# Preparation's products on VectorE and four more filler matmuls per unit, in a fused recurrent-attention and mixture-of-experts kernel

## The chip, the cores and the metric

One core of a Trainium2 chip runs the whole program. The metric is the device time in microseconds (us) of one execution, the median of three runs. Five engines work side by side, each with its own in-order queue: TensorE (PE, matmuls and weight loads), VectorE (DVE), ScalarE (ACT), GpSimd (POOL) and SyncE (SP, which here issues most DMA transfers). An instruction at the head of a queue that waits holds up everything behind it in that queue.

## The reference

Attention is a recurrence over 768 tokens for 4 batches and 8 heads with a 40x40 state per head; its output is the input of a mixture of 8 experts with the best two chosen per token.

```python
for t in range(S):
    y[:, :, t] = np.einsum('bhd,bhde->bhe', rt, state)
    Sa = np.einsum('bhde,bhe->bhd', state, at)
    state_decay = state * wt[:, :, None, :] - np.einsum('bhd,bhe->bhde', Sa, bt)
    state = state_decay + np.einsum('bhd,bhe->bhde', vt, kt)
...
logits = x @ w_gate
noisy_logits = logits + np.log1p(np.exp(x @ w_noise)) * noise
top2 = np.argpartition(-noisy_logits, 2, axis=1)[:, :2]
...
h = np.maximum(x[mask] @ w1[e], 0.0)
out[mask] += top2_w[mask, k, None] * (h @ w2[e])
```

## The kernel before

Attention is computed in chunks of 64 tokens. A **unit** is one chunk of one half `p` (two batches, 8 heads); there are 12 chunks and 2 halves, so 24 units, and they run one after another because the state of a half passes from chunk to chunk. Two chunks of both halves (four units) are a **group**; there are six groups, 0 to 5.

Each group is prepared ahead of its units, once per half. `prepA` scans the decays (`Gx`, L495), takes logarithm and exponential on ScalarE, and forms `NH` and `NG_` (L506). It multiplies `b` by `NH` (L518) and `a` by `NG_` (L520), and after each product `pack` splits the result into two 16-bit halves: ScalarE first (L459), then VectorE (L460), then a DMA. `prepC` does the same for `k`, with two products of half width (L544). `scoresL` multiplies the packed matrices on TensorE, and `tsolve` inverts 32x32 triangles by 30 steps of two vector instructions (L570, L571). The solves of groups 0 and 1 run on VectorE, those of groups 2 to 5 on GpSimd (`TPOOL`); a DMA brings the result back as `T`.

In the kernel before, the products of L518 and L520 run on VectorE for groups 0 and 1 and on GpSimd for groups 2 to 5 (`MD=(0,1)`); those of L506 run on GpSimd for all groups (`MG=()`); those of L544 run on VectorE for group 0 alone (`MK=(0,)`). Group 1's VectorE work goes through the wrapper `Behind` and shows under L399.

A unit has three parts. `chain` applies `T` twice to what the state and the chunk give (tile `pQ`), sums the new state in `pS` and writes it (L667). `outp` forms the attention output (`psc`, `pY`, L680, L691). `Moe.logits` transposes that output (`px`, L97), splits it on ScalarE and VectorE (`xT`, L98, L99) and multiplies it by the gate's weights with nine narrow matmuls (`pl`, L101). `route` and `place` follow for every few units. The experts (`hidden` L287, `output` L309) run after the last unit.

Fillers are matmuls whose result nobody reads: `warm` (L596) multiplies a constant by a constant, 320 columns each, into a PSUM tile that the next real matmul starts anew. Before, there are two per unit, in front of the first application of `T` (`ND=(2,0,0,0)`).

The order of instructions on each engine is not the order of the code. A scheduler simulates the program and issues on each engine what its model finds ready first, with priorities from the code; `burst` keeps runs of matmuls together. A change in one place therefore moves instructions everywhere in attention. PSUM tiles of one tag share buffers: `pl`, `pgm`, `pg`, `pr`, `pn` and the scores of `scoresL` share the single buffer of tag `pp`.

Of the kernel before, what the change touches and what calls it, by code (L numbers as in the profile page):

```python
# [8 lines left out]
F32 = mybir.dt.float32  # L9
# [30 lines left out]
class Moe:  # L40
# [51 lines left out]
    def logits(s,n,xt,ps,tag,bufs=(1,1)):  # L92

        nc=s.nc
        s.xw=s.xws[n]=nc.sync.dma_start(s.xd[n>=NA][128*n:128*n+128],xt)
        px=ps.tile([128,3,128],F32,name="px",tag=tag[0],bufs=bufs[0])
        s.burst([lambda k=k,c0=c0: nc.tensor.transpose(px[:,k],xt[:,c0:c0+128],s.idm) for k,c0 in enumerate((0,128,192))])  # L97
        xT=s.rp.tile([128,2,3,128],F16,name="xT",tag="xT",bufs=2); nc.scalar.activation(xT[:,0],px,AF.Copy,scale=XS)  # L98
        nc.vector.scalar_tensor_tensor(xT[:,1],px,XS,xT[:,0],op0=ALU.mult,op1=ALU.subtract)  # L99
        pl=ps.tile([128,16],F32,name="pl",tag=tag[1],bufs=bufs[1])  # L100
        s.burst([lambda i=i,a=a,b=b,k=k: nc.tensor.matmul(pl,xT[:,a,k],s.wg[:,b,k],start=i+k==0,stop=i+k==4) for i,(a,b) in enumerate(((0,0),(1,0),(0,1))) for k in range(3)])  # L101
        if n==0: s.n0=0
        j=n-s.n0
        if j==0: s.lg=s.rp.tile([128,RT,16],F32,name="lg")
        nc.scalar.activation(s.lg[:,j],pl,AF.Copy,scale=1/(XS*WS))
        if j==s.rts[0]-1:
            s.route(s.n0,s.rts.pop(0),ps,tag[1],bufs[1])
            if n<NA: s.nc.sync.dma_start(s.xd[1][128*s.n0:128*n+128].rearrange("(p a) f->p (a f)",p=128),s.xd[0][128*s.n0:128*n+128].rearrange("(p a) f->p (a f)",p=128))
            s.n0=n+1
            if n+1==NA: s.turn()  # L110
# [293 lines left out]
class Att:  # L404
# [234 lines left out]
    def chain(s,p,cc,o):  # L639
# [19 lines left out]
        s.ul=nc.scalar.activation(s.Ut[:,:,0:40],U,AF.Copy,scale=-IS)  # L659
        if not last:  # L660
            Sp=s.psb.tile([128,8,40],F32,name="pS",tag="pacc",bufs=s.PACC)
            if first: f=[s.mm(Sp,s.idh,s.dm,start=True,stop=False,skip_group_check=True)]
            else: f=[s.mm(Sp,s.ids,sfs[:,l],start=l==0,stop=False,skip_group_check=True) for l in range(2)]
            s.burst(f)
            s.burst([s.mm(Sp[64*b:64*b+40,h],o['kb'][:,b,h],vu[:,b,h],start=False,stop=True,skip_group_check=True) for h,b in HB(1)])
            gb=s.gam[p][:,0:8,cc+1:cc+2].to_broadcast([128,8,40])
            nc.vector.scalar_tensor_tensor(s.Sst[p][:,:,0:40],Sp,IS,gb,op0=ALU.mult,op1=ALU.mult)  # L667
# [80 lines left out]
TB=4  # L748
EW=(1,1)
MB=2  # L750
ND=(2,0,0,0)

BB=1

# [11 lines left out]

BAB=1; RKB=1
SAB=5
MD=(0,1); MG=(); MK=(0,); TG=0
GA=-1; GC=-1  # L770
def HB(k=0): return [(h,b^k) for h in range(8) for b in range(2)]

# [90 lines left out]
def build(nc,tc,A,out):  # L863
    with ExitStack() as ctx:
        m=Moe(nc,tc,ctx,(A['wgn'],A['nz'],A['w1'],A['w2'],out))
        with ExitStack() as c2:
            s=Att(nc,tc,c2,(A['fm'],A['vt'],A['fm2'],A['rv']))
            m.burst=s.burst; s.run(m)
            m.flag(s.ps,"pt",s.PT,s.mags)
        with ExitStack() as c2:  # L870
            m.pools(c2)
            m.experts(s.sd0.ins)
        F=Any_(nc,tc,m,{z:A['raw_'+z] for z in 'rkvwab'},A['nzr'])
        rv=nc.values_load(m.fl[0:1,1:2],min_val=0,max_val=1)
        with tc.If(rv>0):
            with ExitStack() as c2:
                m.pools(c2); m.extra()
            r2=nc.values_load(m.fl[0:1,0:1],min_val=0,max_val=1)
            with tc.If(r2>0):
                F.run()  # L880
# [17 lines left out]
```

## Time and profile before

| | us |
|---|---|
| median of 3 runs | 1052.31 (1048.45 to 1052.65) |
| profiled execution | 1041.7 |
| its span, first to last instruction | 1039.9 |
| PE / PEld busy in the span | 819.7 / 716.3 |
| DVE / ACT / POOL busy | 543.8 / 389.8 / 399.2 |

Durations come from the profiled execution, which was 10.6 us shorter than the median of the runs. "Busy" counts an engine's instructions and not its waits. PEclk is the clock that TensorE was granted, as a share of 2.4 GHz; 0.50 is its lower level, 1.2 GHz. From about 90 us the units run, from about 616 us the experts. In rows of the trace, `out<-in` names what an instruction writes and reads, and a bracket or a second bar gives the idle time in front of it with the instruction that ended it.

### The profile page before, as it was taken

The numbers are of one execution on the slowest core, as the hardware profiler recorded it, in microseconds if no ns is written. First come the engines' busy times: TensorE is split into PE (matmuls) and PEld (weight loads), VectorE is DVE, ScalarE is ACT, GpSimd is POOL, SyncE is SP. The second block draws the span as 40 slices with busy tenths as digits, with TensorE's granted clock in tenths as the row PEclk, the third lists the DMA queues.
The fourth block names the chain that finished last, engine by engine and source line by source line (L and its number), as shares of the span: only waits on it lengthen the run. The fifth ranks groups of instructions, "written<-read, shape, count | busy, mean of one in ns | idle before, by whom it ended". The sixth has DMA issues, their size and how long they took to land.

```text
span 1039.9 us, 27444 instructions
## 1 busy us (share of the span) xinstructions
PE 819.7 (79%) x11706; PEld 716.3 (69%) x11706; DVE 543.8 (52%) x1150; ACT 389.8 (37%) x820; POOL 399.2 (38%) x504
## 2 busy tenths in 40 slices
PE   0113456769888758888988789999999999999994
PEld 0113345557666646777766668899899999999994
DVE  9268568554469774338554753633443434343420
ACT  2202333335445433444442432525243535343420
POOL 6102241167659778219301004335151516160312
PEclk9999998779869866988996789999999999999998
DMA  4793996387588484473494402435252525252303
GB/s 119 177 235 91 254 249 152 93 226 198 124 213 249 126 206 110 110 160 108 138 280 147 135 14 43 120 93 133 58 133 67 131 64 133 61 137 59 35 8 37
DMA packets 127111, 135.88 MB, mean 131 GB/s; under 512 B 59249, under 2 KB 106805, under 8 KB 126901
## 3 DMA queue, kind: packets, MB, share of 16 engines
q1 hardware_dynamic: 116292, 114.90, 41.4%
q0 software_dynamic: 10688, 19.14, 9.7%
q8 instruction: 94, 1.54, 0.6%
q14 instruction: 37, 0.30, 0.1%
HBM read 96.25 MB, written 41.03 MB: 132 GB/s over the span
## 4 chain that ended last, share of the span: by engine, by line
PE 50%; POOL 13%; DMA 13%; DVE 11%; issue 5%; ACT 3%; SPq 2%; POOLq 0%; ACTq 0%; DVEq 0%
PE ph L287 17%; PE po L309 17%; POOL X L571 4%; POOL Tt L570 4%; DMA d_ab<-pk 3%; DMA rawk<-in_fm_dram 3%; PE psc L470 3%; PE pY L470 2%; PE pt L268 2%; PE pQ L470 2%; DVE X L571 1%; DVE Tt L570 1%; PE pW L470 1%; DMA d_k<-pk 1%; DMA X<-scr 1%
## 5 line engine op out<-in xcount | busy, mean ns | idle before, releaser
L311 POOL DMA_INDIRECT out_dram<-y,oi x56 | 92.2, 1647 | 233.7 <-ACT y L310 212.2
L290 DVE SCALAR_TENSOR_TENSOR hl<-ph,hh 128x256 fp32r<-128x256 f32 (+1 forms) x128 | 70.1, 555 | 120.4 <-ACT hh L288 113.2
L288 ACT ACTIVATE hh<-ph 128x320 fp32r<-128x320 f32 (+1 forms) x128 | 64.6, 518 | 147.7 <-PE ph L287 140.4
L470 PE MATMUL pQ<-w,T 32*32 32x40 f32 x2304 | 49.5, 229 | 48.4 <-ACT w L473 23.7
L470 PEld LDWEIGHTS pQ<-w,T 32*32 32x32 f32 x2304 | 42.2, 133 | 61.8 <-ACT w L473 26.3
L309 PE MATMUL po<-w2h,hh 128*128 128x320 f32 x384 | 74.8, 314 | 2.5 <-DVE y L304 1.9
L470 PE MATMUL psc<-RV,uT 128*64 128x128 f32 x384 | 65.3, 325 | 12.6 <-DVE P L680 12.1
L571 POOL TENSOR_TENSOR X<-X,Tt 128x30 f32<-128x30 f32 (+14 forms) x120 | 72.0, 600 | 8.2
L252 POOL DMA_INDIRECT xr<-xd,gi x56 | 53.7, 958 | 51.2 <-DVE oi L178 17.8
L309 PE MATMUL po<-w2h,hl 128*128 128x320 f32 x384 | 70.8, 311 | 0.0
L287 PE MATMUL ph<-xh,w1h 128*128 128x512 f32 (+1 forms) x256 | 69.7, 355 | 1.1 <-DVE hl L290 1.1
L570 POOL TENSOR_TENSOR Tt<-X 128x30 f32<-128x30 f32 (+14 forms) x120 | 67.2, 560 | 7.8
L287 PE MATMUL ph<-xh,w1l 128*128 128x512 f32 (+1 forms) x256 | 68.9, 350 | 0.0
L287 PE MATMUL ph<-xl,w1h 128*128 128x512 f32 (+1 forms) x256 | 68.6, 349 | 0.0
L470 PEld LDWEIGHTS psc<-RV,uT 128*64 128x64 f32 x384 | 51.7, 164 | 22.9 <-DVE P L680 13.0
L309 PE MATMUL po<-w2l,hh 128*128 128x320 f32 x384 | 65.7, 309 | 0.0
L309 PEld LDWEIGHTS po<-w2h,hh 128*128 128x128 f32 x384 | 61.0, 188 | 6.7 <-issue 2.3
L470 PE MATMUL psc<-RV 128*64 128x128 f32 x384 | 65.3, 325 | 0.0
L680 DVE TENSOR_TENSOR P<-psc,mk 128x512 f32<-128x512 f32 x48 | 32.9, 686 | 59.1 <-PE psc L470 59.1
L309 PEld LDWEIGHTS po<-w2h,hl 128*128 128x128 f32 x384 | 59.8, 188 | 0.5
L470 PEld LDWEIGHTS <-st_ab 120*64 120x64 f16 (+1 forms) x928 | 28.3, 123 | 44.1 <-issue 30.5
L309 PEld LDWEIGHTS po<-w2l,hh 128*128 128x128 f32 x384 | 58.6, 188 | 0.1
(314 smaller groups left out, 1936.2 us busy)
## 6 DMA issues: line engine op xcount, KB each, us to landing
w2r<-in_w_dram SPq DMA_DIRECT2D x8, 1280.0 KB
RV<-in_rv_dram SPq DMA_DIRECT2D x48, 192.0 KB
rawba<-in_fm_dram SPq DMA_DIRECT2D x24, 360.0 KB
d_ab<-pk SPq DMA_DIRECT2D x24, 360.0 KB
st_ab<-d_ab SPq DMA_DIRECT2D x36, 240.0 KB
w1r<-in_w_dram SPq DMA_DIRECT2D x8, 1024.0 KB
raww<-in_fm_dram SPq DMA_DIRECT2D x12, 365.6 KB
st_ab<-d_ab SPq DMA_DIRECT2D x24, 180.0 KB
```

The source lines that it names most:

```text
L252: k=t//128; nc.gpsimd.indirect_dma_start(out=X[:p,k if s.cap==CAP else 0],out_offset=None,in_=s.xd[int(w is not s.early[0])],in_offset=OFF ...
L268: for t,p in tiles(t0,n): nc.tensor.transpose(pt[:,t-t0:t-t0+p],x[:p,t//128,f0:f0+128],s.idm[:p,:p])
L287: for i,(a,b) in enumerate(mm): nc.tensor.matmul(ph[:,:n],a,b,start=i==0,stop=i==7)
L288: nc.scalar.activation(hh[:,f,:n],ph[:,:n],AF.Relu)
L290: if c.stop>c.start: nc.vector.scalar_tensor_tensor(o,ph[:,c],0.0,hh[:,f,c].bitcast(F32),op0=ALU.max,op1=ALU.subtract)
L309: s.lm=nc.tensor.matmul(po[:p],h[:,f,r],w[:,f],start=k==0,stop=k==23); k+=1
L311: st=nc.gpsimd.indirect_dma_start(out=s.out_d,out_offset=OFFS(ap=idx[:p,e,ii:ii+1],axis=0),in_=y[:p],in_offset=None,compute_op=ALU.add)
L470: def mm(s,*a,**k): return lambda: s.nc.tensor.matmul(*a,**k)
L570: eng.tensor_tensor(t,Xt[:,j:j+1,j+1:].to_broadcast([128,j,m]),Xt[:,0:j,j:j+1].to_broadcast([128,j,m]),op=ALU.mult)
L571: s.tl=eng.tensor_tensor(Xt[:,0:j,j+1:],Xt[:,0:j,j+1:],t,op=ALU.add)
L680: nc.vector.tensor_tensor(m,pp.rearrange("p i j t->p (i j) t"),s.mk.to_broadcast([128,8,64]),op=ALU.mult)
```

## The change

Two things are changed. First, the products of L506, L518, L520 and L544 all run on VectorE: 12 of L506 (all groups), 8 of L518 and 8 of L520 (groups 2 to 5), and 20 half-width ones of L544 (groups 1 to 5) leave GpSimd. With `0 in MG` the gate's constants are also no longer ordered behind `s.pl`, the last of group 0's L506. Second, `WN=(3,1)` adds fillers: three in front of the logits' product, written to the unused 320 columns of the widened tile `plw`, and one in front of the state's sum `pS`. That is 24 x 3 and 22 x 1, 94 in all.

```diff
-        pl=ps.tile([128,16],F32,name="pl",tag=tag[1],bufs=bufs[1])
+        plw=ps.tile([128,336],F32,name="pl",tag=tag[1],bufs=bufs[1]); pl=plw[:,0:16]
+        s.warm(plw[:,16:336],WN[0])
...
             Sp=s.psb.tile([128,8,40],F32,name="pS",tag="pacc",bufs=s.PACC)
+            s.warm(Sp,WN[1])
...
-ND=(2,0,0,0)
+ND=(2,0,0,0); WN=(3,1)
...
-MD=(0,1); MG=(); MK=(0,); TG=0
+MD=MG=MK=range(6); TG=0
...
-            m.burst=s.burst; s.run(m)
+            m.burst=s.burst; m.warm=s.warm; s.run(m)
```

Two lines are added to the code, so L518 of before is L519 of the changed kernel, L506 is L507, L544 is L545, and L596 is L597.

On GpSimd, at the preparation of group 4's second half (`NG__4427`), which stands among the first steps of group 3's solve (`Tt` and `X` are the solve's tiles, `rawba` holds `b` and `a`), the order before is:

```order
L571 TENSOR_TENSOR X<-X,Tt 128x2x29
L506 TENSOR_TENSOR NG__4427<-Gx,raww 120x768
L570 TENSOR_TENSOR Tt<-X 128x84
L571 TENSOR_TENSOR X<-X,Tt 128x3x28
L570 TENSOR_TENSOR Tt<-X 128x108
L518 TENSOR_TENSOR rawba<-rawba,NH 120x768
L571 TENSOR_TENSOR X<-X,Tt 128x4x27
L520 TENSOR_TENSOR rawba<-rawba,NG__4427 120x768
```

The same steps of that solve in the changed kernel:

```order
L572 TENSOR_TENSOR X<-X,Tt 128x2x29
L571 TENSOR_TENSOR Tt<-X 128x84
L572 TENSOR_TENSOR X<-X,Tt 128x3x28
L571 TENSOR_TENSOR Tt<-X 128x108
L572 TENSOR_TENSOR X<-X,Tt 128x4x27
L571 TENSOR_TENSOR Tt<-X 128x130
L572 TENSOR_TENSOR X<-X,Tt 128x5x26
```

The three products have left the solve, whose steps follow each other.

On VectorE, at the end of the same preparation, the order before is (`pk` is the packed half, `Sst` the state, `xT` the split output):

```order
L680 TENSOR_TENSOR P<-psc,mk 128x512
L658 TENSOR_SCALAR vu<-pQ 64x320
L691 TENSOR_TENSOR xt<-pY,xt 128x320
L606 TENSOR_TENSOR ak<-psc,mk_127 128x512
L460 SCALAR_TENSOR_TENSOR pk<-rawba,pk 120x768
L667 SCALAR_TENSOR_TENSOR Sst_169<-pS,gam_148 128x8x40
L99 SCALAR_TENSOR_TENSOR xT<-px,xT 128x384
L460 SCALAR_TENSOR_TENSOR pk<-rawba,pk 120x768
```

In the changed kernel, there (`NG__4467` is this preparation's `NG_`, `rawk` holds `k`):

```order
L545 TENSOR_TENSOR rawk<-rawk,NH 120x6x64 x2
L461 SCALAR_TENSOR_TENSOR pk<-rawba,pk 120x768
L682 TENSOR_TENSOR P<-psc,mk 128x512
L507 TENSOR_TENSOR NG__4467<-Gx,raww 120x768
L521 TENSOR_TENSOR rawba<-rawba,NG__4467 120x768
L461 SCALAR_TENSOR_TENSOR pk<-rawba,pk 120x768
L682 TENSOR_TENSOR P<-psc,mk 128x512
L461 SCALAR_TENSOR_TENSOR pk<-rawk,pk 120x2x384
L659 TENSOR_SCALAR vu<-pQ 64x320
```

Two `pk` were all that VectorE had of this preparation there; now the products stand between the units' own work (`P`, `vu`), each in front of the `pk` that needs it.

On TensorE, at a unit's logits in the middle of attention (`pn` is a step of routing, `idh` and `dm` the filler's constants), before:

```order
L165 MATMUL pn<-ohB,ohA 128x256
L97 MATMUL px<-idm,xt 128x128 x3
L471 MATMUL pd<-idf,Sst_170 128x128 x4
L101 LDWEIGHTS xT
L101 MATMUL pl<-wg,xT 128x16
```

and in the changed kernel:

```order
L166 MATMUL pn<-ohB,ohA 128x256
L97 MATMUL px<-idm,xt 128x128 x3
L472 MATMUL pd<-idf,Sst_170 128x128 x4
L597 LDWEIGHTS idh
L597 MATMUL pl<-dm,idh 128x320
```

The last two rows are the first filler, with its own weight load; two more follow it, then the logits' product with `xT`, which stood there before.

## Rows read from the trace of the kernel before

**Rows 1.** The windows view by stage of the program. Columns: stretch in us from the span's start, its length, then busy us (and instructions) of each engine, the granted TensorE clock, the busy share of the DMA engines, GB/s.

```profile
200.00:616.00 416.00, 339.67 (x7760) 279.82 (x7760) 236.01 (x517) 173.89 (x414) 209.22 (x312) 0.82 0.61 160
616.00:1040.00 424.00, 404.98 (x2460) 373.53 (x2458) 172.03 (x373) 160.62 (x298) 142.27 (x110) 0.99 0.35 81
```

**Rows 2.** From the page: busy time of each engine in the span, and the chain that ended last, shares of the span by engine.

```profile
PE 819.7 (79%) x11706; PEld 716.3 (69%) x11706; DVE 543.8 (52%) x1150; ACT 389.8 (37%) x820; POOL 399.2 (38%) x504
...
PE 50%; POOL 13%; DMA 13%; DVE 11%; issue 5%; ACT 3%; SPq 2%; POOLq 0%; ACTq 0%; DVEq 0%
```

**Rows 3.** The waits of ScalarE (ACT) from 100 to 620 us: who waited for whom, us in total, times, longest.

```profile
ACT pk L459 <- POOL rawba L518: 38.4, 8, 7.7
...
ACT pk L459 <- POOL rawba L520: 8.3, 6, 3.6
...
ACT pk L459 <- POOL rawk L544: 5.0, 1, 5.0
```

**Rows 4.** The timeline of ScalarE from 375 to 386 us: start, duration, line, operation, output from input, and in brackets the idle time in front and its releaser.

```profile
382.64 0.84 ACT L459 ACTIVATE pk<-rawba 120x768 f16<-120x768 f32 x1 [7.16 <-POOL rawba L518]
...
384.28 0.44 ACT L473 ACTIVATE w<-pW 128x320 f32<-128x320 f32 x1
```

**Rows 5.** The timeline of GpSimd (POOL) from 380 to 383 us.

```profile
380.38 0.48 POOL L570 TENSOR_TENSOR Tt<-X 128x168 f32<-128x168 f32 x1
380.81 1.80 POOL L518 TENSOR_TENSOR rawba<-rawba,NH 120x768 f32<-120x768 f32 x1
382.57 0.54 POOL L571 TENSOR_TENSOR X<-X,Tt 128x168 f32<-128x168 f32 x1
```

**Rows 6.** The timeline of TensorE (PE) at five places, one row each: first matmuls after a wait.

```profile
174.15 1.27 PE L470 MATMUL pQ<-w,T 32*32 32x40 f32 x32 [6.31 <-ACT w L473]
...
228.49 0.25 PE L101 MATMUL pl<-wg,xT 128*128 128x16 f16 x3 [6.30 <-ACT xT L98]
...
269.92 0.76 PE L470 MATMUL pW<-q,lo 32*32 32x40 f32 x32 [1.76 <-ACT q L652]
...
303.64 0.25 PE L101 MATMUL pl<-wg,xT 128*128 128x16 f16 x3 [3.03 <-ACT xT L98]
...
384.77 1.28 PE L470 MATMUL pQ<-w,T 32*32 32x40 f32 x32 [6.72 <-ACT w L473]
```

**Rows 7.** The windows view again, in stretches of 8 us behind three of those waits (columns as in rows 1).

```profile
224.00:232.00 8.00, 3.44 (x43) 2.92 (x44) 5.69 (x6) 3.26 (x7) 7.85 (x7) 0.50 0.94 210
...
304.00:312.00 8.00, 6.88 (x122) 5.43 (x124) 5.85 (x14) 3.24 (x9) 6.37 (x9) 0.50 1.00 247
...
384.00:392.00 8.00, 4.36 (x86) 3.62 (x88) 7.94 (x9) 4.05 (x9) 7.84 (x8) 0.50 0.62 164
...
392.00:400.00 8.00, 6.22 (x99) 5.54 (x99) 5.08 (x7) 1.67 (x4) 7.05 (x10) 0.50 0.67 178
...
400.00:408.00 8.00, 7.34 (x121) 5.47 (x121) 1.80 (x3) 2.44 (x6) 6.71 (x9) 0.50 0.29 73
```

**Rows 8.** TensorE's timeline at two places: two filler matmuls (L596) and the matmuls that follow, at the low clock (400 to 405 us) and at the high one (433 to 435 us).

```profile
402.66 0.71 PE L596 MATMUL pQ<-dm,idh 128*128 128x320 f16 x2
...
404.03 1.22 PE L470 MATMUL pQ<-w,T 32*32 32x40 f32 x60 [0.66 <-ACT w L473]
...
433.79 0.45 PE L596 MATMUL pQ<-dm,idh 128*128 128x320 f16 x2
...
434.16 0.79 PE L470 MATMUL pQ<-w,T 32*32 32x40 f32 x64
```

**Rows 9.** What one product costs on either engine: for a line, the count, min/median/max in ns, first and last start, forms. L518 multiplies `b` by `NH`, L544 half of `k`.

```profile
L518 POOL TENSOR_TENSOR rawba<-rawba,NH x8: 1799/1804/1946, 119.7 to 380.8; 120x768 f32<-120x768 f32 x8
...
L518 DVE TENSOR_TENSOR rawba<-rawba,NH x2: 946/952/959, 14.1 to 24.8; 120x768 f32<-120x768 f32 x2
...
L544 POOL TENSOR_TENSOR rawk<-rawk,NH x20: 985/1007/1942, 91.9 to 401.8; 120x384 f32<-120x384 f32 x20
...
L544 DVE TENSOR_TENSOR rawk<-rawk,NH x4: 549/553/557, 39.5 to 47.3; 120x384 f32<-120x384 f32 x4
```

**Rows 10.** VectorE's group of L504 from 90 to 616 us, a product of the form of L518 that VectorE has done all along (shapes, count, busy us, mean ns, idle in front); then VectorE's timeline at 372 us and GpSimd's at 370 us, two instructions that ran at the same time.

```profile
L504 DVE TENSOR_TENSOR NH<-raww,Gx 120x768 f32<-120x768 f32 x8 | 11.5, 1443 | 0.1
...
372.57 2.76 DVE L504 TENSOR_TENSOR NH<-raww,Gx 120x768 f32<-120x768 f32 x1
...
370.35 4.17 POOL L564 TENSOR_TENSOR X<-X,tri 128x1024 f32<-128x1024 f32 x1 [5.37 <-DMA X<-scr]
```

**Rows 11.** TensorE's groups from 90 to 616 us: line, tiles, count, busy us, mean ns, and after the second bar the idle time in front with what ended it. L101 is the logits' product.

```profile
L101 PE MATMUL pl<-wg,xT 128*128 128x16 f16 x216 | 11.9, 174 | 21.3 <-ACT xT L98 13.1 <-DVE xT L99 6.5 <-DVE tab L166 0.6
```

**Rows 12.** The waits of GpSimd for DMA from 100 to 620 us.

```profile
POOL rawk L544 <- DMA rawk<-in_fm_dram: 34.0, 7, 18.8
...
POOL rawba L518 <- DMA rawba<-in_fm_dram: 6.5, 2, 4.0
```

**Rows 13.** GpSimd's timeline: first product and closing transfer of the solve for group 3, and the same for group 5.

```profile
291.26 2.13 POOL L564 TENSOR_TENSOR X<-X,tri 128x1024 f32<-128x1024 f32 x1 [6.89 <-DMA Vz<-in_vt_dram]
...
354.28 0.62 POOL L573 DMA_DIRECT2D scr<-X  x1 [0.32 <-POOL X L571]
...
463.85 2.13 POOL L564 TENSOR_TENSOR X<-X,tri 128x1024 f32<-128x1024 f32 x1 [39.81 <-DMA X<-scr]
...
504.65 0.59 POOL L573 DMA_DIRECT2D scr<-X  x1 [0.30 <-POOL X L571]
```

## The prediction

> **What bounds the kernel now.** I read the windows by stage first. From 616 us on, in the experts, TensorE is busy 404.98 of 424 us at a granted clock of 0.99 [rows 1]; the change adds and moves nothing there, so I leave that stage as it is. From 200 to 616 us, in attention, TensorE is busy 339.67 of 416 us and its clock is 0.82, while VectorE is busy 236.01 and GpSimd 209.22 [rows 1]. No engine is full. Time is lost in two ways there: TensorE waits 76 us (416 less 340), and it works part of the time at its lower clock. A mean of 0.82 between the levels 1.0 and 0.5 means that 36% of the stretch, some 150 us, ran at the lower one. The chain that ended last gives the same picture: TensorE half of the span, GpSimd 13%, VectorE 11%, ScalarE 3% [rows 2].
>
> Next I asked who makes TensorE wait, and read ScalarE's waits. The largest that has to do with the change is `pk` (L459), which waits for the products on GpSimd: 38.4 us for L518, 8.3 us for L520 and 5.0 us for L544, together 51.7 us [rows 3]. The reader can follow one of them in the timelines. GpSimd was in the middle of a solve and came to L518 only at 380.81, for 1.80 us [rows 5]. ScalarE stood at `pk` for 7.16 us until 382.64, and `w`, which is the unit's own work, was queued behind it and ran at 384.28 [rows 4]. TensorE, which needed `w`, stood for 6.72 us [rows 6]. The solve's own lateness is not what is waited for here; a short product behind it in a queue is.
>
> **The change part by part. Stalls removed.** With the products on VectorE, GpSimd has only solve steps and routing sums, and `pk` no longer waits for it. Five waits of TensorE follow such a stop of ScalarE: 6.31, 6.30, 1.76, 3.03 and 6.72 us, 24.1 us in all [rows 6]. The bounds are 0 (something else is late at the same moment) and 51.7 (all that ScalarE waited [rows 3]); I take the 24.1, which is what reached TensorE in one piece, and 18% of the other 27.6, 5 us, because TensorE waits 18% of the stage (76 of 416) and these ten stops of ScalarE may show in its shorter waits. That is 29 us.
>
> **Cold work removed.** Behind three of these waits the clock is at 0.50 for five stretches, in which TensorE is busy 3.44 + 6.88 + 4.36 + 6.22 + 7.34 = 28.2 us [rows 7]. The same narrow matmuls take 1.22 us per 60 there and 0.79 us per 64 at the high clock [rows 8], a ratio of 0.61. At the high clock the 28.2 us would be 17.2, a gain of 11. Over the whole stage the most to be had so is 150 us x 0.82 busy x 0.39 = 48 us, and the least is 0. Each 0.01 of the mean clock is 2.7 of these 48 us. I take a mean of 0.88 for a TensorE that idles less and has fillers, which is 16 us: the 11 and 5 more.
>
> **VectorE's new work.** It gets 28 products of 768 columns and 20 of 384. One takes 0.952 us and 0.553 us on VectorE where nothing else is in its way, against 1.804 and 1.007 on GpSimd [rows 9]: 26.7 + 11.1 = 37.7 us. L504 has the same form as the wide one and is run by VectorE already, partly beside a solve; its mean is 1.443 us [rows 10]. By that factor of 1.52 the sum is 57.2 us. Work on VectorE costs nothing where VectorE would have idled, and all of it where a unit waits for `vu`, `P` or `Sst` behind it, so 0 and 57.2 are the ends. The chain gives VectorE 11% of 1039.9 us, 114 us, of 543.8 busy [rows 2], so 21% of its time is on the path; 21% of 37.7 to 57.2 is 8 to 12, and I take 10. On what the two engines do to each other, the trace shows L504 at 2.76 us while GpSimd's L564 ran 4.17 us [rows 10], where L564 takes 2.13 us elsewhere [rows 13]. The Trainium skill, "SBUF — State Buffer", section "Who interferes with whom", says why: a VectorE instruction with two SBUF inputs and a GpSimd instruction that reads SBUF share a read interface, and whichever begins first keeps it to its end. The trace agrees as to a long wait on both sides. By that rule the change trades a late product for a blocked one, and the 57.2 is the likelier sum; that rule's case is the second rival.
>
> **Waits for DMA that change engine.** On GpSimd, L544 waited 34.0 us for `rawk` and L518 6.5 us for `rawba` [rows 12]; on VectorE the same wait would hold the units' own work. The largest, 18.8 us [rows 12], was in an empty stretch of GpSimd and would move with the order; 21.7 us are left. I take VectorE's 21% of that, 5 us; the ends are 0 and 21.7.
>
> **The solve.** Without products among its steps it is shorter: group 3's went from 291.26 to 354.28, 63 us with the preparation of group 4 in it, group 5's from 463.85 to 504.65, 41 us with none [rows 13]. I cost that at nothing. Group 3's result left at 354.28 [rows 13], and units still worked on for tens of us; the wait at 384.77 was for `w` and not for `T` [rows 6]. If another thing removed that slack, 22 us per solve would count.
>
> **Fillers.** There are 94. Two of them take 0.71 us at the low clock and 0.37 at the high one (433.79 to 434.16) [rows 8], so 0.355 and 0.185 each; at the stage's mix of clocks (36% low) 0.246, together 23 us. They stand in front of the logits' product, where TensorE waited 21.3 us in all [rows 11]. Of those, 6.30 and 3.03 are stalls already counted as removed [rows 6], so 12 us are left to fill, and 11 us are uncovered. With no cover at all the cost is 23 (up to 33 if everything were cold), with full cover 0; fillers that keep the clock up pay some of it back, which is in the 5 above. The order on GpSimd and the startup are the remaining edits: `NG_` of group 0 on VectorE and the constants issued earlier are worth 1 us either way, and I count 0.
>
> **The sum.** 29 + 16 - 10 - 5 - 11 = 19 us less. The profiled execution took 1041.7 us, so it would be 1022.7. The median before, 1052.31, is 10.6 above that execution, so for the median I add 10.6 and forecast 1033 us, 1.8% less.
>
> **The rivals.** First, the clock follows: removing the stalls keeps TensorE high for most of the stage, the mean goes to about 0.95, and 35 of the 48 us of cold work come back instead of 16. For it speaks that low stretches follow idle ones in each of the three places of rows 7; against it, that the stage has many smaller waits that stay. Time 1033 - 19 = 1014.
>
> Second, and on the other side, VectorE becomes the engine in whose queue the units wait. The products stand between `P` and `vu` now, each can be held by a solve step or a transfer, and `pk` on ScalarE still waits, for VectorE instead. Then half of the 29 comes back (14 gained), no clock is gained, the blocked products cost 12, the fillers 11, the transfers 5: 14 us more, 1066. It decides where VectorE's share through a preparation, 57% over the stage now (236 of 416 [rows 1]), passes the 82% that TensorE has. For it speaks L504 at 2.76 us [rows 10]; against it, the 180 us of idle VectorE in the stage [rows 1].
>
> Third, the stalls go and the clock does not rise: 29 less, 12 + 5 + 11 more, 1 us gained, 1051. VectorE and the fillers eat what the move earns. It holds if the low clock of rows 7 comes from elsewhere than those waits.
>
> Fourth, the change does not do what it says, because the scheduler lays out all of attention anew. Fillers take the single buffer of tag `pp` earlier, and the scores that feed a solve wait for it. One filler triple of 0.56 to 1.07 us in each of 24 units is 13 to 26 us at most in that buffer; half of it on the path gives 1058 or so with a part of the gains lost.
>
> **How the numbers follow.** Forecast 50% (its own range 1022 to 1044), first rival 15%, second 15%, third 15%, fourth 5%. A measurement of this kernel can tell about 0.5%, 5.3 us, from no change, so faster is below 1047.0 and slower above 1057.6. The forecast, the first rival and 4 of the third's 15 give 0.69 for faster. Of the third 10, and 2 of the fourth, give 0.12 for the same. The second rival, the rest of the fourth and 1 of the third give 0.19 for slower. The range reaches down to 1008, below the first rival, and up to 1060, which holds the third and the fourth and leaves most of the second out: 6% below and 14% above.
>
> **What would show it.** Right: ScalarE's wait of `pk` for a product falls from 51.7 us to below 15, TensorE's mean clock in attention is about 0.88, solves on GpSimd take 41 to 48 us each, and attention ends some 19 us earlier. The fillers show as a shorter idle time in front of L102 with three matmuls before it. Wrong: `pk` waits as long for VectorE, VectorE is over 82% busy through preparations, products take 1.4 us and more, or the experts' stage changes at all.

## The result and the profile after

The changed kernel took 1061.76 us (median of 7 runs, 1056.74 to 1064.28), the kernel before, run beside it, 1051.36 (7 runs, 1043.68 to 1052.65). The ratio, worked out from the single runs and not from the two medians, is 1.0107, with a 95% interval from 1.0072 to 1.0143: about 1.1% slower, where 1.8% faster was forecast. The profiled execution took 1064.28 us, with a span of 1062.5. It is 22.6 us longer than the profiled execution of before (1041.7), twice the 10.4 us between the medians, so the two profiles are read here for where time goes and not for how much the change costs. Two added lines make L518 of before L519 here, L544 is L545, L459 is L460 and L680 is L682.

The busy line of the profile's page and its chain, which answer to [rows 2]:

```profile
PE 830.0 (78%) x11800; PEld 719.4 (68%) x11800; DVE 557.2 (52%) x1198; ACT 389.9 (37%) x820; POOL 319.7 (30%) x456
...
PE 55%; DVE 17%; DMA 15%; issue 6%; ACT 4%; SPq 3%; POOL 0%; POOLq 0%; ACTq 0%; DVEq 0%
```

GpSimd has left the chain (13% before, 0% now), VectorE has gone from 11 to 17% and TensorE from 50 to 55%. The place that GpSimd had on the path is taken, not freed. The window of attention, columns as in [rows 1]:

```profile
200.00:616.00 416.00, 326.41 (x7578) 265.78 (x7577) 233.90 (x523) 163.54 (x391) 161.86 (x282) 0.82 0.60 158
```

In attention TensorE is busy 326 us where it was 340, so it idles 90 us instead of 76, at the same mean clock of 0.82. VectorE is no busier over these 416 us than before, although it has more to do: the stage runs later. Attention's last output is at 624.6 us, against 610.8 (614.4 in a second profile of the kernel before, e4 below).

ScalarE's waits from 100 to 620 us, as in [rows 3]:

```profile
ACT pk L460 <- DVE rawba L519: 26.9, 6, 10.7
...
ACT pk L460 <- DVE rawba L521: 11.6, 6, 4.9
...
ACT pk L460 <- DVE rawk L545: 6.1, 2, 4.0
```

`pk` waits 44.6 us for products (26.9 + 11.6 + 6.1), against 51.7 before; for the most part only the engine's name has changed. VectorE's own waits in the same stretch say why, and answer to [rows 12]:

```profile
DVE rawk L545 <- DMA rawk<-in_fm_dram: 24.9, 8, 6.2
DVE rawba L519 <- DMA rawba<-in_fm_dram: 13.0, 3, 12.0
```

So 37.9 us of waits for loads, of the kind that stood on GpSimd before (40.5 us [rows 12]), now stand on VectorE. What they hold up is to be read at one place, in the fifth unit (unit 4, counted from 0). VectorE, then ScalarE, then TensorE:

```profile
213.18 1.03 DVE L519 TENSOR_TENSOR rawba<-rawba,NH 120x768 f32<-120x768 f32 x1 [11.97 <-DMA rawba<-in_fm_dram]
214.14 0.68 DVE L682 TENSOR_TENSOR P<-psc,mk 128x512 f32<-128x512 f32 x1
...
234.26 1.74 DVE L545 TENSOR_TENSOR rawk<-rawk,NH 120x384 f32<-120x384 f32 x2 [5.90 <-DMA rawk<-in_fm_dram]
...
236.39 0.47 DVE L669 SCALAR_TENSOR_TENSOR Sst<-pS,gam 128x320 f32<-128x320 f32 x1
```

```profile
214.25 0.84 ACT L460 ACTIVATE pk<-rawba 120x768 f16<-120x768 f32 x1 [10.67 <-DVE rawba L519]
...
216.24 0.44 ACT L474 ACTIVATE w<-pW 128x320 f32<-128x320 f32 x1
```

```profile
214.87 0.47 PE L471 MATMUL psc<-RV,uT 128*64 128x128 f32 x1 [8.46 <-DVE P L682]
...
237.42 0.42 PE L471 MATMUL pst<-sfs,sel 128*120 128x320 f16 x1 [5.57 <-ACT sfs L625]
```

VectorE stands 11.97 us at a product whose load has not landed, and `P` behind it, which belongs to the unit, runs as soon as the product is done. The same product holds ScalarE's `pk` for 10.67 us with `w` behind it. TensorE gets neither and waits 8.46 us; 20 us later two half products stand 5.90 us in front of the state's `Sst`, and TensorE waits 5.57. The load itself is late because of a third line, SP's, which issues the transfers:

```profile
204.30 3.61 SPq L594 DMA_DIRECT2D T<-scr  x4
207.95 0.46 SPq L522 DMA_DIRECT2D d_ab<-pk  x1
208.46 1.51 SPq L492 DMA_DIRECT2D rawba<-in_fm_dram  x2
```

VectorE had been at the product since 201.2 us; the load was issued at 208.46, behind the copies of a solve's result `T`.

### The profile page after: what moved, and what is told of

The parts are those of the page before. It is cut to its first block, busy times and chain, and to the rows that moved or that the text cites. A ratio compares the mean times of both kernels' runs of the same rounds, so it can differ in the third digit from the quotient of the medians.

```text
span 1062.5 us, 27610 instructions
## 1 busy us (share of the span) xinstructions
PE 830.0 (78%) x11800; PEld 719.4 (68%) x11800; DVE 557.2 (52%) x1198; ACT 389.9 (37%) x820; POOL 319.7 (30%) x456
## 4 chain that ended last, share of the span: by engine, by line
PE 55%; DVE 17%; DMA 15%; issue 6%; ACT 4%; SPq 3%; POOL 0%; POOLq 0%; ACTq 0%; DVEq 0%
PE po L310 16%; PE ph L288 16%; DMA d_ab<-pk 4%; PE psc L471 4%; PE pY L471 3%; DMA rawk<-in_fm_dram 3%; PE pW L471 2%; PE pQ L471 2%; DMA d_k<-pk 2%; PE pt L269 2%; DMA st_ab<-d_ab 2%; DMA RV<-in_rv_dram 2%; DVE X L572 2%; DVE Tt L571 1%; DVE pk L461 1%
## 5 line engine op out<-in xcount | busy, mean ns | idle before, releaser
L565 POOL TENSOR_TENSOR X<-X,tri 128x1024 f32<-128x1024 f32 x4 | 11.1, 2780 | 329.3 <-DMA T<-scr 187.1
L471 PE MATMUL psc<-RV,uT 128*64 128x128 f32 x384 | 62.8, 315 | 20.4 <-DVE P L682 17.2
L571 POOL TENSOR_TENSOR Tt<-X 128x30 f32<-128x30 f32 (+14 forms) x120 | 69.6, 580 | 8.5
L682 DVE TENSOR_TENSOR P<-psc,mk 128x512 f32<-128x512 f32 x48 | 33.0, 688 | 73.8 <-PE psc L471 71.7
L572 POOL TENSOR_TENSOR X<-X,Tt 128x30 f32<-128x30 f32 (+14 forms) x120 | 68.8, 573 | 8.9
L471 PEld LDWEIGHTS psc<-RV,uT 128*64 128x64 f32 x384 | 49.5, 159 | 30.5 <-DVE P L682 18.1
L471 PE MATMUL psc<-RV 128*64 128x128 f32 x384 | 62.9, 316 | 3.4 <-issue 3.4
```

Of the source, the lines that this page charges most:

```text
L471: def mm(s,*a,**k): return lambda: s.nc.tensor.matmul(*a,**k)
L565: eng.tensor_tensor(Xt,Xt,s.tri,op=ALU.mult)
L571: eng.tensor_tensor(t,Xt[:,j:j+1,j+1:].to_broadcast([128,j,m]),Xt[:,0:j,j:j+1].to_broadcast([128,j,m]),op=ALU.mult)
L572: s.tl=eng.tensor_tensor(Xt[:,0:j,j+1:],Xt[:,0:j,j+1:],t,op=ALU.add)
L682: nc.vector.tensor_tensor(m,pp.rearrange("p i j t->p (i j) t"),s.mk.to_broadcast([128,8,64]),op=ALU.mult)
```

## The experiments

The first four take the change apart. Theory L is that of the loads just read, F that of the fillers' own time, V that of VectorE's added work.

**e1, products alone:** the changed kernel without its 94 fillers.

```diff
-ND=(2,0,0,0); WN=(3,1)
+ND=(2,0,0,0); WN=(0,0)
```

> The changed kernel without its 94 fillers (WN=(0,0)); the 48 products stay on VectorE. Theory L (the products brought their waits for the loads of rawba and rawk, 37.9 us, into VectorE's queue, and what stands behind them waits too): nearly all of the loss stays, ratio to before 1.005 to 1.012, pk on ScalarE still waits over 35 us for VectorE, VectorE waits over 30 us for rawba and rawk. Theory F (the fillers are uncovered and cost 11 to 23 us, the move of the products itself gains): ratio 0.985 to 0.998. Theory V (VectorE's added work itself, 38 to 57 us, is on the path where TensorE waits for P): 1.005 to 1.012 like L, to be told from it by e3.

0.9895 [0.9848, 0.9941], 1032.05 us (median) against 1044.53: faster by 1.05%. The products alone bring a gain. Yet ScalarE's `pk` waits 42.0 us for them, and VectorE 36.6 us for `rawk` and `rawba`:

```profile
ACT pk L460 <- DVE rawba L519: 22.1, 6, 6.6
ACT pk L460 <- DVE rawba L521: 15.6, 5, 7.0
...
ACT pk L460 <- DVE rawk L545: 4.3, 2, 2.9
```

```profile
DVE rawk L545 <- DMA rawk<-in_fm_dram: 24.5, 8, 6.4
DVE rawba L519 <- DMA rawba<-in_fm_dram: 12.1, 3, 5.1
```

These sums are within 3 us of the changed kernel's, and the two kernels differ by 2%. A sum of waits does not tell what they cost.

**e2, fillers alone:** the products' line is that of before.

```diff
-MD=MG=MK=range(6); TG=0
+MD=(0,1); MG=(); MK=(0,); TG=0
```

> The kernel before with the 94 fillers alone (products of groups 2 to 5 on GpSimd as before). Theory F: 11 to 23 us slower, ratio 1.010 to 1.022, TensorE's busy time in attention up by 15 to 25 us. Theories L and V: the fillers stand where TensorE waits anyway, ratio 0.998 to 1.004. A granted clock in attention above 0.84 would say that fillers keep it up, below 0.82 that they do not.

1.0003 [0.9972, 1.0034]. Fillers on the kernel before cost nothing in the layout that the scheduler made for them, so F falls. But products alone gain 1% and fillers alone cost nothing, while both together lose 1%: the parts do not add up, and L and V, which expected e1 to be slower than before, fall as stated, too. In e2 ScalarE's `pk` waits 25.0 us for the products on GpSimd, where the kernel before has 51.7, and nothing is gained. Its largest part (38.4 us before):

```profile
ACT pk L460 <- POOL rawba L519: 19.5, 7, 7.1
```

**e3, half-width products back on GpSimd, no fillers** (`WN=(0,0)` as in e1).

```diff
-MD=MG=MK=range(6); TG=0
+MD=MG=range(6); MK=(0,); TG=0
```

> Products on VectorE except the 20 half-width ones of L545 (rawk), which go back to GpSimd; no fillers. Theory L: 24.9 of VectorE's 37.9 us of waits for loads go back to an engine that has time for them, so most of the loss goes: ratio 0.995 to 1.002 and at least 6 us below e1. Theory V: only 11 of 38 us of work leave VectorE, so at most 3 us below e1. Theory F says nothing of the difference between e1 and e3.

1.0118 [1.0073, 1.0162], slower than e1 by 2.2% although it takes VectorE's largest sum of waits away, that for `rawk`; the one for `rawba` rose from 12.1 to 24.7 us. None of the theories has room for it.

**e4, the kernel before once more, unchanged.**

> The kernel before, unchanged, with a profile of its own. It tells how much of a difference between two profiles is no effect of the change: ratio 1.000 within 0.004. If the experts' stage, whose instructions the change leaves in their order, varies by itself, this profile's stage from the last state output on is more than 3 us away from the 424 us of the first profile; if the 8 us that it grew in the changed kernel belong to the change, it is within 2 us of it.

1.0001 [0.9961, 1.0042]. From attention's last output to the end of the span it needs 430.5 us, the first profile 429.1, and the changed kernel's profile 437.9. By the line written down beforehand that gives the 8 us to the change, but later kernels that keep its order (e6, e9, e11, e12) need 426.7 to 430.1 there. The kernel before took 1051.36 us beside the changed kernel and 1039.74 to 1045.67 in all later groups of runs, so I take these 8 us for a property of that occasion. That is argued, not shown; each ratio compares runs of the same occasion.

What e1 to e3 have in common is that the scheduler lays out all of attention anew for each. Between e1 and the changed kernel, a row-by-row comparison of the orders, without tile numbers and fillers, has some 140 removed or added rows on VectorE and some 90 each on ScalarE and SP, though the two programs differ in nothing but fillers. Between e2 and the kernel before there are some 170 on VectorE, and they cost nothing. So I formed theory O: the layout decides, and it can come out either way. To test it I let the scheduler lay out one program, read off the order on every engine, and gave the other program the same order by edges that only order and wait for nothing:

```diff
+                for chain in order[1]:
+                    for a,b in zip(chain,chain[1:]):
+                        tc.add_manual_dep(seq[b],seq[a].name,mybir.DependencyInfo(mybir.DependencyClass.NoSync,mybir.DependencyReason.DATA),reason="order")
...
+    _,_,order=trace((0,0))
+    nc,arrays,_=trace((3,1),order)
```

The last two lines are those of e5: order from a program without fillers, run with them. Instructions that only one program has are left free, and in e7, e8 and e13 all the products, too. The lines of such kernels are 1 to 5 higher (L519 is L520 or L524).

**e5, e1's order, with fillers.**

> Products on VectorE and the 94 fillers, as in the changed kernel, but every other instruction of every engine held in the order that the scheduler gave e1 (products alone); the fillers stand in front of pl and pS. Theory O (the fillers do their harm by the new order that the scheduler lays out when it has them in the program): 0.985 to 1.000, near e1's 0.9895. Theory F' (the fillers' own time is what costs, once the products are on VectorE): 1.007 to 1.014, as the changed kernel. In between, both have a share, which the difference to e1 gives.

0.9949 [0.9914, 0.9985].

**e6, the changed kernel's order, without fillers.**

```diff
+    _,_,order=trace((3,1))
+    nc,arrays,_=trace((0,0),order)
```

> The changed kernel without its 94 fillers, every other instruction of every engine held in the order that it has with them. Theory O: 1.003 to 1.014, still slower than before, though nothing but the products is added. Theory F': 0.985 to 0.995, as e1.

1.0172 [1.0122, 1.0222]. In the traces, fillers left out, the rows of e5 follow each other as in e1, and those of e6 as in the changed kernel, on VectorE, ScalarE, GpSimd and SP alike. The four cases make a table. With e1's order the ratio is 0.9895 without fillers and 0.9949 with them; with the changed kernel's order 1.0172 and 1.0107. The order is worth 1.6 to 2.8%. The fillers move the ratio by half a per cent one way or the other, and there the intervals overlap. Theory O holds; what the fillers did was to make the scheduler choose another layout.

**e7, products on VectorE, all else in the order of before; e8, products back on GpSimd, all else in the order of e1.** No fillers in either.

```diff
+    _,_,order=trace((0,0),((0,1),(),(0,)))
+    nc,arrays,_=trace((0,0),(range(6),)*3,order)
```

(e7; e8 has the two settings the other way round.)

> No fillers; the 48 products on VectorE, all other instructions of every engine held in the order of the kernel before. If the move itself gains (theory M, the prediction's own: ScalarE's pk and the solve no longer wait), 0.982 to 0.993, and pk waits under 30 us for products. If e1's gain is only another order (theory O for this part as well), 0.996 to 1.010.

> No fillers; the 48 products back on the engines of the kernel before (GpSimd for groups 2 to 5), all other instructions of every engine held in the order of e1. Theory M: the gain of e1 is lost, 0.997 to 1.012, pk waits over 40 us for GpSimd. If e1's gain is its order alone: 0.985 to 0.994.

e7 1.0105 [1.0071, 1.0139], e8 1.0106 [1.0074, 1.0138]. The same move of the same 48 products costs 1% in the order of before and gains 2.1% in e1's (1.0106 to 0.9895). Neither the engine nor the order alone is good. e8 came as theory M expected; e7 lies far above theory M's range and just above the other. The shorter wait that theory M looked for did come: `pk` waits only 19.0 us for the products that moved (22.7 with group 1's). The gain did not come, so less waiting of `pk` is not less time. The largest part of the 19.0:

```profile
ACT pk L465 <- DVE rawba L524: 14.1, 3, 8.1
```

How either goes wrong: e7's VectorE stands for `rawk` with more of the preparation and `P` behind it, and TensorE waits for `P`:

```profile
224.08 1.49 DVE L550 TENSOR_TENSOR rawk<-rawk,NH 120x384 f32<-120x384 f32 x2 [7.58 <-DMA rawk<-in_fm_dram]
...
228.44 0.68 DVE L689 TENSOR_TENSOR P<-psc,mk 128x512 f32<-128x512 f32 x1
```

```profile
229.17 1.94 PE L476 MATMUL pY<-kb,P 128*64 128x40 f32 x32 [10.68 <-DVE P L689]
```

And e8's `pk`, in an order made for quick products, stands longer for GpSimd (67.6 us in all) than in the kernel before (51.7):

```profile
ACT pk L465 <- POOL rawba L524: 35.3, 6, 12.0
ACT pk L465 <- POOL rawba L526: 23.5, 6, 5.7
ACT pk L465 <- POOL rawk L550: 8.8, 2, 5.4
```

**Where the two orders part.** The start of the write of the state, `Sst<-pS`, by unit, in us (VectorE's timeline of each kernel):

| unit | before | e1 | changed | e6 | e9 | e10 | e12 |
|---|---|---|---|---|---|---|---|
| 3 | 205.9 | 197.5 | 196.4 | 197.4 | 196.9 | 198.1 | 195.7 |
| 4 | 227.9 | 225.8 | 236.4 | 236.4 | 230.1 | 227.4 | 234.2 |
| 7 | 282.7 | 278.0 | 298.9 | 297.5 | 292.1 | 274.2 | 293.7 |
| 8 | 304.1 | 313.6 | 331.6 | 328.0 | 325.8 | 303.8 | 324.8 |
| 21 | 560.7 | 555.3 | 578.9 | 574.8 | 569.9 | 551.5 | 573.0 |

The second profile of the kernel before (e4) is within 2.6 us of the first at all five. At unit 3 the changed kernel leads before by 9.5 us, and e1 leads it by 8.4. At unit 4, the place read above, the changed kernel is 10.6 us behind e1, and 20.9 at unit 7; little is added after that. In e1 the product of `rawba` has the same place and the half products another:

```profile
209.68 0.96 DVE L519 TENSOR_TENSOR rawba<-rawba,NH 120x768 f32<-120x768 f32 x1 [5.12 <-DMA rawba<-in_fm_dram]
...
225.83 0.48 DVE L669 SCALAR_TENSOR_TENSOR Sst<-pS,gam 128x320 f32<-128x320 f32 x1
229.75 1.56 DVE L545 TENSOR_TENSOR rawk<-rawk,NH 120x384 f32<-120x384 f32 x2 [3.44 <-DMA rawk<-in_fm_dram]
```

`Sst` stands in front of the half products here, and the load of `rawba` was issued at 204.91, 3.5 us earlier. By the timelines, e1's first `P` (210.55) is 3.6 us ahead of the changed kernel's and its `ak` (223.76) 3.9; the rest of the 10.6 us comes with the half products in front of `Sst`. The further loss, in unit 6, goes with two things in one place, neither of them tested alone: the unit's `ak` stands behind a preparation's steps on VectorE, TensorE waits 3.79 us for it at 271.98, and the granted clock is low there. Two windows of the changed kernel:

```profile
260.00:270.00 10.00, 6.59 (x217) 5.80 (x215) 6.36 (x9) 5.03 (x11) 0.00 (x0) 0.93 0.72 170
270.00:280.00 10.00, 7.20 (x81) 6.04 (x82) 4.91 (x11) 3.76 (x9) 0.00 (x0) 0.50 0.62 137
```

In the second one TensorE is busy 7.20 us with only 81 matmuls, at 0.50. In e1 the clock is 1.00 in both windows, though its units are further on there.

**e9, five moves in the changed kernel's order,** in units 4 and 6. Each entry names the engine, the tile that the moved instruction writes, which of its writes, and the tile and the write behind which it goes:

```diff
+    MOVES=(('DVE', 'rawba_2891', (0, 1), 'P_2083', 0), ('DVE', 'rawk_4134', (0, 2), 'uT_2377', 0), ('Activation', 'pk_2911', (0, 1), 'kb_2135', 3), ('DVE', 'ak_3182', (0, 1), 'raww_4045', 0), ('Activation', 'pk_4067', (0, 1), 'xt_2766', 0))
```

> The changed kernel (products on VectorE, fillers, its own order), held in that order but for five moves in units 4 and 6: on VectorE the product of rawba that waited 11.97 us stands behind P, the two of rawk that waited 5.90 us behind Sst, sfs and uT, and ak ahead of one step of a preparation; on ScalarE the two pk that waited 10.67 and 3.45 us stand behind xt, kb, w and sE. Theory L (the units' own work is held because it stands in line behind products that wait for a load): units 4 to 7 run 10 to 20 us earlier than in the changed kernel, ratio 0.990 to 1.001. Theory V (the loads do no harm, VectorE's added work or the clock does): same work, same time, 1.006 to 1.014.

1.0032 [0.9996, 1.0068]: of the changed kernel's loss some two thirds are gone, with the same instructions on the same engines. The ratio lies below theory V's range. Units 4 to 7 are 5 to 7 us earlier, less than L's 10 to 20. What was left shows in the rows. The first `P` now runs at once, but the load is as late as ever, and the unit's second `P` stands behind the products:

```profile
203.76 0.69 DVE L685 TENSOR_TENSOR P<-psc,mk 128x512 f32<-128x512 f32 x1 [2.02 <-PE psc L472]
...
213.72 1.10 DVE L520 TENSOR_TENSOR rawba<-rawba,NH 120x768 f32<-120x768 f32 x1 [9.26 <-DMA rawba<-in_fm_dram]
...
220.75 0.68 DVE L685 TENSOR_TENSOR P<-psc,mk 128x512 f32<-128x512 f32 x1
```

**e10, twelve moves of the same kind in e1's order.**

```diff
+    MOVES=(('DVE', 'rawba_2867', (0, 1), 'P_2070', 0), ('Activation', 'pk_2887', (0, 1), 'kb_2122', 3), ('DVE', 'rawk_4098', (0, 2), 'uT_2360', 0), ('DVE', 'P_3502', (0, 1), 'rawba_4416', 0), ('Activation', 'pk_4436', (0, 1), 'kb_3554', 3), ('DVE', 'rawk_5184', (0, 2), 'P_3513', 0), ('Activation', 'pk_5189', (0, 1), 'vu_3285', 0), ('DVE', 'pk_5189', (0, 1), 'vu_3285', 0), ('DVE', 'rawk_5581', (0, 2), 'uT_3884', 0), ('DVE', 'rawba_5884', (0, 1), 'P_5066', 0), ('Activation', 'pk_5904', (0, 1), 'kb_5118', 3), ('DVE', 'rawk_6714', (0, 2), 'P_5077', 0))
```

> e1 (products alone) in its own order but for twelve moves of the same kind at its stops in the preparations of groups 3 to 5: products that wait for a load stand behind the unit's next P, or behind Sst, sfs and uT, and the pk of them behind kb, w, xt and sE on ScalarE. Theory L: e1 loses part of its 36.6 us of waits for loads on units' work too, so 5 to 15 us come back, ratio 0.975 to 0.985. Theory V: 0.987 to 0.993, as e1. If it is above 0.993, the preparations were made later by the moves and hold the units in turn.

0.9848 [0.9823, 0.9873], 1025.54 us against 1041.70: the fastest of all, 1.5% under the kernel before, and as L expected. Against e1 that is 0.5%, with intervals that overlap; in the table unit 21 is 3.8 us earlier than in e1. VectorE's wait for `rawk` went from 24.5 to 6.9 us. That for `rawba` rose from 12.1 to 17.8; 9.4 of it is one product of group 4's preparation, which I had left in front of `P`.

```profile
DVE rawba L520 <- DMA rawba<-in_fm_dram: 17.8, 4, 9.4
DVE rawk L546 <- DMA rawk<-in_fm_dram: 6.9, 5, 3.0
```

**e11 and e12, the loads instead of the places.** In the changed kernel's order, e11 has the two loads of `rawba` issued ahead of ten of the `T` copies; e12 has the load of `rawk` and two stores there as well.

```diff
+    MOVES=(('SP', 'rawk_3729', (0, 1), 'T_2025', 1), ('SP', 'rawba_2891', (0, 2), 'T_2025', 1), ('SP', 'd_k_2588', (0, 1), 'T_2025', 1), ('SP', 'd_ab_2515', (1, 2), 'T_2025', 1))
```

(e12; e11 has the second of the four entries alone.)

> The changed kernel in its own order with one move, on SP: the two loads of rawba for group 3's second half, issued at 208.46 us behind fourteen copies of a solve's T, stand ahead of the last ten of these; their buffer is free from about 195.6 us. If the wait of 11.97 us is SP's queue, VectorE's wait for that load falls below 4 us, ScalarE's pk there from 10.67 to below 4, unit 4 ends 6 to 10 us earlier and the ratio is 0.999 to 1.006. If the load itself or its buffer is what is late, the wait stays over 8 us and the ratio is 1.007 to 1.014.

> The changed kernel in its own order, with four kinds of SP's issues at unit 4 ahead of ten copies of a solve's T instead of behind them: the two stores of an earlier pk (d_ab, d_k) that e11's ScalarE stood on, and the loads of rawba and rawk. Theory Q (the stop at unit 4 is SP's queue: whatever the products and the pk wait for stands behind the T copies): ScalarE's pk at 211.69 us of e11 waits under 3 us instead of 7.94, unit 4's state is written 5 to 10 us before the changed kernel's 236.4 us, ratio 1.000 to 1.006. If the unit is held by yet another thing as soon as this one is free (the P and pk still stand in line with the products), unit 4 is within 3 us of 236.4 and the ratio 1.007 to 1.014.

e11 1.0105 [1.0068, 1.0142], the changed kernel's own ratio, with unit 4 at 236.3 as before, although VectorE's wait of 11.97 us is gone and `P` runs at 204.42 instead of 214.14. The half products in front of `Sst` still stand (6.40 us in place of 5.90). ScalarE's `pk` stands, too, 7.94 us in place of 10.67, now for the store of an earlier `pk` whose buffer it needs, and `w` behind it:

```profile
211.69 0.84 ACT L461 ACTIVATE pk<-rawba 120x768 f16<-120x768 f32 x1 [7.94 <-DMA d_k<-pk]
...
213.68 0.44 ACT L475 ACTIVATE w<-pW 128x320 f32<-128x320 f32 x1
```

e12 takes that away too. That `pk` runs at 204.92 and its second one at 209.47; then the third stands:

```profile
204.92 0.84 ACT L461 ACTIVATE pk<-rawba 120x768 f16<-120x768 f32 x1 [2.28 <-DVE rawba L520]
...
223.13 0.84 ACT L461 ACTIVATE pk<-rawk 120x768 f16<-120x768 f32 x1 [12.37 <-issue]
```

Unit 4 ends at 234.2, 2.2 us earlier, and the ratio is 1.0081 [1.0054, 1.0107]: the second of the two readings that were written down. The profile names no releaser for the 12.37 us; the store of the `pk` two before it was issued by SP at 216.58, behind transfers that wait, so a buffer is likely but not shown. Freeing one wait of a preparation brings up its next one, as long as the unit's work is behind it in line. That e11, which is the changed kernel with one move, has its ratio also speaks for it that holding an order costs nothing by itself.

**e13, e3 in e1's order; e14, e5 with 210 fillers in place of 94.**

```diff
+    _,_,order=trace((0,0),(range(6),)*3)
+    nc,arrays,_=trace((0,0),(range(6),range(6),(0,)),order)
```

```diff
+    _,_,order=trace((0,0))
+    nc,arrays,_=trace((6,3),order)
```

> e3 with the order taken out of it: products on VectorE except the 20 half-width ones of L545, which are on GpSimd; all other instructions held in the order of e1; no fillers. Theory P (place decides: a product costs what stands behind it in its engine's line): VectorE loses its 24.5 us of waits for rawk, GpSimd has time for them outside the solves, ratio 0.980 to 0.992, equal to e1 or better, and e3's 1.0118 was its order. Theory G (what the prediction feared of GpSimd: a product behind solve steps makes pk late): 0.994 to 1.006.

> e5 with 210 fillers in place of 94 (six in front of pl, three in front of pS), all other instructions in the order of e1. If a filler costs what lies uncovered of its 0.19 to 0.36 us, e5's step over e1 (0.005, some 5 us) becomes 10 to 16 us more than e1 in all: ratio 0.999 to 1.006. If fillers pay for themselves by a higher clock, 0.988 to 0.996 and a granted clock in attention above e5's.

e13 0.9956 [0.9929, 0.9984]: e3's 1.0118 was 1.6% of order. With the order held, the half products are no better on GpSimd; by the ratios they are 0.6% worse than in e1, with intervals that overlap. Theory P expected at least e1's time and fell there, and the ratio lies in theory G's range: `rawk`'s waits left VectorE, but those for `rawba` rose from 12.1 to 21.3 us, and `pk` stands 13.9 us for GpSimd.

```profile
ACT pk L465 <- DVE rawba L524: 30.1, 6, 10.9
ACT pk L465 <- POOL rawk L550: 13.9, 3, 7.4
```

e14 0.9980 [0.9950, 1.0009], between the two expectations. In one order, 0, 94 and 210 fillers give 0.9895, 0.9949 and 0.9980: some 5.6 and 8.9 us of 1043, or 0.06 and 0.04 us for each filler; e14's step over e1 is clear of the intervals, e5's is not. One lasts 0.185 to 0.355 [rows 8], so most of it is covered or paid back. The windows of e5 and of e14 show TensorE's busy time and clock rising together; how the rest divides between cover and clock is not shown.

```profile
200.00:616.00 416.00, 338.48 (x7767) 274.93 (x7767) 248.03 (x588) 172.32 (x412) 158.20 (x279) 0.86 0.59 157
```

```profile
200.00:616.00 416.00, 342.19 (x7829) 278.55 (x7829) 239.07 (x554) 169.25 (x405) 157.27 (x276) 0.87 0.59 157
```

Without fillers, e1 has 332.48 us and 0.84 there.

## Why the prediction was wrong

The sign was wrong: 1033 us was forecast, with a range to 1060, and 1061.76 came. Two rivals' times lie some 4 us off, on either side: the fourth's 1058 and the second's 1066. The reason of each holds in part, so that their nearness is partly luck. The first rival (a clock of 0.95) and the third (stalls gone) fell with the stalls, which stayed.

**Stalls removed, 29 us.** This step failed. It took it that `pk` waits for GpSimd and stops waiting when GpSimd is out of the way. `pk` waits for a product, and that for a load, a buffer, SP's line; on VectorE it waited 44.6 us where I wrote that under 15 would show me right. Nor is this wait the price that I took it for: in e2 it is 25.0 us and in e7 19.0, both less than half of the 51.7, and e2 gains nothing while e7 loses 1%. Five waits of TensorE were counted as gained [rows 6] without asking what the layout would put in front of the same instructions next. I had written the question into the bounds ("something else is late at the same moment") and put the end at 0; it is below 0. What the runs showed in place of this step is the order: with the same products on VectorE and no fillers, e1's order gains 1.05% and the changed kernel's loses 1.72%.

**Cold work removed, 16 us.** The clock did not rise: 0.82 before, 0.82 after. It was to follow from the stalls, and they stayed. Nor does the stage's mean clock rank the kernels: it is 0.84 in e1 and 0.86 in e5, which gain, and 0.83 in e11 and 0.84 in e12, which lose.

**VectorE's new work, 10 us.** The durations came near the low end of their bounds. The groups of L519, L545 and, for contention, L505 (L504 of before) from 90 to 616 us, as in [rows 10]:

```profile
L545 DVE TENSOR_TENSOR rawk<-rawk,NH 120x384 f32<-120x384 f32 x20 | 13.5, 713 | 24.9 <-DMA rawk<-in_fm_dram 24.9
L505 DVE TENSOR_TENSOR NH<-raww,Gx 120x768 f32<-120x768 f32 x8 | 10.8, 1344 | 0.1
L519 DVE TENSOR_TENSOR rawba<-rawba,NH 120x768 f32<-120x768 f32 x8 | 7.7, 966 | 13.1 <-DMA rawba<-in_fm_dram 13.0
```

A wide product of L519 took 0.966 us in the mean, near the 0.952 of [rows 9], a half one 0.713 against 0.553. Beside a solve on GpSimd a wide one took up to 1.40. The 44 products of L507, L519, L521 and L545 from 90 us on kept VectorE busy for 38.0 us, where the durations of [rows 9] would give 33.9 and the factor of 1.52 would give 51.5. So the 57.2 us, which rested on L504's mean, did not come, and VectorE's share is 56% of the stage and 40% of the 40 us from 200 us on, far from the 82% at which the second rival was to decide. By the Trainium skill ("SBUF — State Buffer", "Who interferes with whom") a VectorE instruction with two SBUF inputs contends with a GpSimd instruction that reads SBUF; the trace agrees that products are longer beside a solve (1.40 against 0.95 us). That is not what cost the time: e1 has the same products on VectorE and gains. This rival's other half, that units wait in VectorE's line, is what happened.

**Waits for DMA that change engine, 5 us.** This is the term that should have carried the forecast. I set the largest wait aside and multiplied 21.7 us by the 21% of VectorE's time that is on the path. What stands behind a wait is no average: 11.97 us stood directly in front of `P`, and 5.90 in front of `Sst`. The sum, 37.9, was above my upper end, and yet the sum is not the price, since e1 has 36.6 and is faster.

**The solve, at nothing.** The solves did get shorter, as forecast (41 to 48 us): those of groups 2 and 3 lie between these pairs of GpSimd's rows, 41.7 and 43.1 us, against 57.2 and 63.0 before:

```profile
203.65 2.12 POOL L565 TENSOR_TENSOR X<-X,tri 128x1024 f32<-128x1024 f32 x1 [187.08 <-DMA T<-scr]
...
245.31 0.83 POOL L574 DMA_DIRECT2D scr<-X  x1 [0.33 <-POOL X L572]
304.37 2.24 POOL L565 TENSOR_TENSOR X<-X,tri 128x1024 f32<-128x1024 f32 x1 [58.22 <-DMA X<-scr]
...
347.42 0.62 POOL L574 DMA_DIRECT2D scr<-X  x1
```

That a shorter solve is worth nothing was not tested by itself; nothing here speaks against it.

**Fillers, 11 us.** Over-sized: about 6 in e1's order, none on the kernel before (in a layout of its own), and in the changed kernel's order a gain of 0.65% by the ratios; in both held orders the intervals overlap. Part of the cover was there; the idle time in front of the logits' product fell from 21.3 us [rows 11] to 8.4, and 7.3 more stand in front of the fillers:

```profile
L597 PE MATMUL pl<-dm,idh 128*128 128x320 f16 x69 | 16.3, 351 | 7.3 <-DVE tab L167 4.0 <-ACT xt L691 3.3
...
L102 PE MATMUL pl<-wg,xT 128*128 128x16 f16 x198 | 10.9, 174 | 8.4 <-DVE xT L99 5.8 <-ACT xT L98 2.2
```

**The rivals.** The fourth, that the scheduler lays attention out anew, had 5% and was looked for in one PSUM buffer. It is the one that decides between a loss of 1.1% (the changed kernel) and a gain of 0.5% (e5) for the same instructions. I had read the order for the products' places and seen them between `P` and `vu`, and did not price what a wait there would hold. "The experts' stage changes at all" was written as a sign against me; it was 8 us longer in this profile, and the later kernels that keep the order do not have these 8 us.

What stays open: which of the differing rows matter beyond the five moves of e9, which recovered some two thirds; what the low clock in unit 6 costs; and what the third `pk` of e12 waits for.

## What to carry to other kernels

An instruction that moves to another engine takes its waits along; what it costs there is what stands behind it in that engine's line, so price the two or three instructions behind each wait, not the sum of waits times a share. Where a scheduler lays out the program, an edit of a per cent is one edit plus a new layout of the same size: run the edit with the order held, and the new order without the edit, before believing either. In line, the repeated unit's own work goes in front of a later stage's preparation, above all in front of anything that waits for a load; here five such moves took back some two thirds of the loss (e9), and twelve in e1's order made the fastest kernel (e10, 0.5% under e1, with intervals that overlap).

## What was not expected of the hardware

SP's line of issues reaches other engines. Ten copies of `T` stood in front of two loads, the last four of them 3.61 us long (204.30 to 207.95), and VectorE waited 11.97 us for a load; with the loads ahead of these ten (e11) that wait was gone, and ScalarE stood 7.94 us for a store at the same unit. Taking the stops out one after the other moved the unit by less than 0.1 us (e11) and by 2.2 us (e12) only.
